# A software-pipelined FFT-and-MLP kernel: small products moved behind the next product with P, a group's swap moved behind the doubled copy

## The chip, the cores and the metric

The kernel runs on one core of a Trainium2 chip. Five engines have a part in it: TensorE (PE, with its weight loads shown as a row of their own, PEld), VectorE (DVE), ScalarE (ACT), GpSimd (POOL) and SyncE (SP), whose queue issues nearly all DMAs. The metric is the device time of one execution in microseconds; of several runs the median is taken. One run was also profiled, and its trace is what all durations here come from.

## The reference

Eight sequences of 3008 rows by 256 columns go through a two-dimensional FFT, of which the real part is kept; the result, 24064 rows, goes through a two-layer network with the gate `h * sigmoid(1.702 h)` between the layers.

```python
X = np.fft.fft(x, axis=1)          # x: (8, 3008, 256) float32
X = np.fft.fft(X, axis=2)
x = X.real.astype(np.float32).reshape(24064, 256)
h = x @ w_in                       # w_in: (256, 2048)
g = h * (1.0 / (1.0 + np.exp(-1.702 * h)))
out = (g @ w_out)                  # w_out: (2048, 256), all float32
```

## The kernel before, in words

**Tiles.** The FFT along the 3008 rows is split as 47 by 64. `fold1` (POOL, lines 225 to 231) adds mirrored halves of the input, `mix1` (PE, line 255) makes the 47-point transforms, `mixed` (ACT, line 263) copies their sums back into `xt`, `spill` and `fill` turn the data through memory, and `stage2` (PE, line 365, then DVE transposes, line 371) makes the 64-point part. The FFT along the 256 columns is folded into the weights `wcs`. What `stage2` leaves is `pqt[b, blk]`, with two halves, P (index 0) and Q (index 1). A row k and its mirror image share P and differ in the sign of Q, so both are had from one product with P and one with Q. Below, `mix1` and `stage2` together are called transforms.

**Steps and slots.** A step t is one quadruple (b, blk, hh, p): 8 sequences, 3 blocks of 512 rows, 2 halves of 256 rows (226 in the second half of the first block), and 8 pairs p of 128-wide chunks of the 2048 hidden features. There are 384 steps; the 8 steps of one (b, blk, hh) are a group, and each has its own output sums. The main loop (lines 989 to 1082) makes one pass, a slot, for each t. From t = 8 on, a slot issues on each engine the next piece of several steps at once, and the order in the source is the order in each engine's queue. There is no scheduler.

Slot t of the kernel before issues:

- On PE: `begin(t, 1)`, the product of step t with Q (line 184, `x`); the first part of the output product of step t - 3 (`product`, line 184, `o`); `begin(t + 1)`, the product of step t + 1 with P; the rest of the output product. Around these lie the small products (line 685): a second level of the fast 2-by-2 block product, made once for two steps. One slot of every two has those numbered 1, 2, 4, 7 (`one`), the other those numbered 5, 6, 3 (`other`).
- On ACT: `forward(t)` (line 607, the gate of the direct rows, from PSUM); in one slot of eight `swap` (lines 794 to 796, three copies of 64 partitions that exchange parts of a finished group's sums); `doubled(t + 1)` (line 604, the copy 2x of the product with P, before Q is added); `activate_back(t)` (line 614, the gate of the mirrored rows); `middle(t + 2)` (line 592, two activations that put the start value into the PSUM bank of x).
- On DVE: `backward(t)` (line 565, the mirrored rows, made from `doubled` and x); in odd or even slots `sums` (lines 629, 630) or `deeper` (line 651); and for a finished group `combine` (757, 758), `combine_small` (786), `combine_last` (768, 804) and two turns (737, each followed by stores on SP).
- On POOL: `sums(t, nc.gpsimd)` (lines 622, 623) and, where a slot has one, a part of `fold1`.

x has two PSUM banks, `b0` and `b1`, by the parity of t. A transform at the end of slot t borrows the bank of step t. It therefore has to wait for `forward(t)` and `backward(t)`, and `middle(t + 2)` cannot be issued in that slot: the code calls the slot `special`. The next slot, called `after`, starts with that `middle` on ACT, ahead of `forward`. There `begin(t + 1)` waits for a `middle` that was issued only a moment ago, and the kernel before puts three parts of the output product and the first small product in front of it. 51 slots are `after` slots. `begin(t, 1)` in turn waits for `doubled(t)`, which must have read the PSUM bank.

A group's last step is t0 with p = 7. In slot t0 + 3 `combine` runs, in t0 + 4 `combine_small`, in t0 + 5 (there the current step has p = 4) `swap` on ACT and `combine_last` on DVE, and in t0 + 6 and t0 + 7 the two turns with their stores. 46 groups have a swap.

The lines around the change:

```python
            product(t - LAG, 0, cut)
            if after:
                small_products(one[0], one[1][:1])
                small_products(other[0], () if opening else other[1][:1])
            if t + 1 < n:
                begin(t + 1)
...
            small_products(one[0], one[1][after:])
            swap(t - LAG - 2)
            if t < n:
                backward(t)
            if t + 1 < n:
                doubled(t + 1)
```

Of the kernel before, what the change touches and what calls it, by code (L numbers as in the profile page):

```python
# [43 lines left out]
LAG = 3  # L44
# [68 lines left out]
def kernel(ctx: ExitStack, tc, x, w_in, w_out, tab1, tab2, out):  # L113
# [471 lines left out]
    def middle(t):  # L585

        b, blk, hh, p = steps[t]
        n = width(t)
        x = xb[t] = bank("x", f"b{t % 2}")
        for i in range(2):  # L590
            f = 2 * p + i
            nc.scalar.activation(x[:, i * 256:i * 256 + n], nbt[b, blk][:, hh * 256:hh * 256 + n], ACTF.Copy,  # L592
                                 scale=af1[:, f:f + 1])
# [194 lines left out]
    def swap(t):  # L788

        if not group_end(t):  # L790
            return
        n = width(t)
        one, two_, kept = (free(big[lo:lo + 64], RES + at, [512, 2], [1, n]) for lo, at in ((64, 0), (0, 256), (64, 1024)))
        nc.scalar.copy(kept, two_)
        nc.scalar.copy(two_, one)
        nc.scalar.copy(one, kept)
# [192 lines left out]
    for t in range(n + LAG):  # L989
        if t < NP:  # L990
            if t == NP - 3:
                spare[:] = [tag for tag in spare if tag[0] == "o"] + ["b2"]
            if t == NP - 1:
                middle(NP)
            hidden(t)
            if t == NP - 1:
                begin(NP)
                no_row(1024)
            if t == 0:
                squares(in2, nc.scalar)  # L1000
                nyquist(0, 0)
                low_up(in2)
                low_down(in2)
            if t in rows_at:
                first_row(rows_at[t])
            if t >= LAG and t != LAG + 1:
                product(t - LAG, 0, None)
            if t == LAG:
                product(1, 0, None)
            if t == 5:  # L1010
                bounds(("out", 2))
            if t == 6:
                low_down(("out", 3))
            if t:
                activate(t - 1)
            if t == 3:
                bounds(("in", 3))
            if t == 5:
                bounds(("out", 3), False)
            if t in early:  # L1020
                fold_w(early[t])
            rows(t)
            if t == NP - 1:
                doubled(NP)
                middle(NP + 1)
        else:
            after, special = (any(fn in (mix1, stage2) for fn, _ in extra.get(k, ())) for k in (t - 1, t))
            if t < n:
                begin(t, 1)
            if t == NP:  # L1030
                activate(t - 1)
            if after and t + 1 < n:
                middle(t + 1)
            if t < n:
                forward(t)
            while waiting:
                m, ps = waiting.pop()
                mixed(m, 1, ps)
            opening = (t - LAG) % NP == 0 and t >= NP + LAG
            one, other = (t - LAG, (1, 2, 4, 7)), (t - LAG - 1, (5, 6, 3))  # L1040
            if opening:
                small_products(*other)
            cut = 0 if opening and not after else 3 if after else 2
            product(t - LAG, 0, cut)
            if after:
                small_products(one[0], one[1][:1])
                small_products(other[0], () if opening else other[1][:1])
            if t + 1 < n:
                begin(t + 1)
            if not opening:  # L1050
                small_products(other[0], other[1][after:])
            product(t - LAG, cut, 6 if t - LAG == last else None)
            small_products(one[0], one[1][after:])
            swap(t - LAG - 2)
            if t < n:
                backward(t)
            if t + 1 < n:
                doubled(t + 1)
            if t < n:
                activate_back(t)  # L1060
                sums(t, nc.gpsimd)
            if t + 2 < n and not special:
                middle(t + 2)
            combine_small(t - LAG - 1)
            if t - LAG == last:
                product(last, 6, None)
            sums(t - 1, nc.vector)
            deeper(t - 2, 0)
            deeper(t - 3, 1)
        if t == NP:  # L1070
            psu.close()
            low = ctx.enter_context(tc.tile_pool(name="low", bufs=1, space=PS))
            pot["low"] = low.tile([128, 3 * 512], F32, tag="low", name="low")
        if t >= LAG:
            combine(t - LAG)
            combine_last(t - LAG - 2)
            turn_last(t - LAG - 3, 0)
            turn_last(t - LAG - 4, 1)
        if t >= NP:
            spare[:] = [f"b{t % 2}"] * special + ["b2"]  # L1080
        for fn, args in extra.get(t, ()):
            fn(*args)
# [28 lines left out]
```

## Time and profile before

| | |
|---|---|
| median of 3 runs | 1855.01 us (1854.38 to 1855.89) |
| the profiled execution's own time | 1854.86 us |
| its span, first to last instruction | 1853.1 us |
| PE busy | 1836.6 us, 99% of the span |
| PEld busy | 1401.3 us, 76% |
| DVE busy | 1520.9 us, 82% |
| ACT busy | 1150.5 us, 62% |
| POOL busy | 975.2 us, 53% |
| granted TensorE clock, mean | 0.999 |

Busy time is the time in which an engine had at least one instruction under way. A line of the timeline gives the start in microseconds from the start of the span, the time from there to the end, the engine, the line of the source, the operation, the tiles written and read, the shape and the number of instructions put together; in brackets stands the idle time of the engine before it and what ended that. A line of the list of waits reads: who waited, for whom, microseconds in total, how often, the longest. fp32 matmuls are recorded in two passes, so that one `begin` of four matmuls shows as x8.

### The profile page before, as it was taken

Reading aid. Unit: us, or ns where it says so; the run is one execution under the profiler, and the core shown is the slowest. Engines: PE = TensorE matmul, PEld = TensorE weight load, DVE = VectorE, ACT = ScalarE, POOL = GpSimd, SP = SyncE. Lnnn points to the kernel's source line nnn. Section 1 sums busy time; section 2 is a strip of 40 time slices with the busy share of each in tenths; the row PEclk is TensorE's granted clock in tenths of the full one; section 3 lists DMA queues with packets and bytes.
Section 4 is the critical chain, followed back from the end, with each engine's and each line's share of the span. In section 5 each row is a group of like instructions: output and inputs, shape, how many; then the busy total and the mean of one; then the engine's idle time right before and its main releaser. Section 6 shows DMA issues by size and latency. Waiting matters only on the chain.

```text
span 1853.1 us, 56093 instructions
## 1 busy us (share of the span) xinstructions
PE 1836.6 (99%) x23722; PEld 1401.3 (76%) x23722; DVE 1520.9 (82%) x2222; ACT 1150.5 (62%) x2241; POOL 975.2 (53%) x1053
## 2 busy tenths in 40 slices
PE   8999999999999999999999999999999999999998
PEld 4677777777777777777777777777777777778776
DVE  6988778887798778987789878888888888878874
ACT  5666656665666666666566666666665666656663
POOL 4776446744368434773348643485445754444442
PEclk9999999999999999999999999999999999999999
DMA  8721340215012240223302132121411111100111
GB/s 280 181 61 34 85 67 19 72 52 99 19 46 48 73 81 13 52 50 90 57 13 67 43 86 52 19 75 35 103 31 23 37 46 36 31 19 13 23 19 24
DMA packets 149707, 105.31 MB, mean 57 GB/s; under 512 B 106057, under 2 KB 130665, under 8 KB 148896
## 3 DMA queue, kind: packets, MB, share of 16 engines
q1 hardware_dynamic: 146624, 99.68, 23.6%
q8 instruction: 187, 3.06, 0.7%
q10 hardware_dynamic: 2832, 2.05, 0.5%
q14 instruction: 64, 0.52, 0.1%
HBM read 64.41 MB, written 48.05 MB: 61 GB/s over the span
## 4 chain that ended last, share of the span: by engine, by line
PE 80%; DVE 9%; POOL 4%; ACT 2%; DMA 2%; issue 2%; SPq 0%; DVEq 0%; ACTq 0%; POOLq 0%
PE x L184 29%; PE o L184 22%; PE low L685 21%; PE o L685 3%; DVE big L651 3%; PE ps L255 2%; DVE big L786 2%; DVE big L565 1%; PE ps L365 1%; POOL xt L227 1%; DVE big L629 1%; POOL big L623 1%; DMA xt<-in_x_dram 1%; ACT big L607 1%; DMA Td<-big 1%
## 5 line engine op out<-in xcount | busy, mean ns | idle before, releaser
L622 POOL TENSOR_TENSOR big<-big 128x256 f32<-128x256 f32 (+1 forms) x376 | 353.0, 939 | 825.1 <-ACT big L614 691.4
L184 PE MATMUL x<-pq,wcs 128*64 128x256 f32 (+1 forms) x6016 | 768.8, 376 | 2.0 <-ACT g L604 1.4
L651 DVE TENSOR_TENSOR big<-big 128x512 f32<-128x512 f32 (+1 forms) x736 | 623.1, 861 | 23.4 <-PE low L685 4.7
L184 PE MATMUL o<-big,wo 128*64 128x256 f32 (+1 forms) x4800 | 620.8, 375 | 0.1
L184 PEld LDWEIGHTS x<-pq,wcs 128*64 128x64 f32 x6016 | 412.3, 137 | 186.0 <-issue 15.0
L184 PEld LDWEIGHTS o<-big,wo 128*64 128x64 f32 x4800 | 341.6, 137 | 148.0 <-DVE big L629 0.5
L604 ACT ACTIVATE g<-x 128x512 f32<-128x512 f32 (+1 forms) x376 | 221.6, 589 | 366.3 <-PE x L184 365.0
L565 DVE TENSOR_TENSOR big<-g,x 128x512 f32<-128x512 f32 (+2 forms) x440 | 254.1, 589 | 209.4 <-ACT big L607 209.0
L592 ACT ACTIVATE x<-nb,af 128x256 f32<-128x256 f32 (+1 forms) x752 | 352.9, 469 | 79.7 <-DVE pq L371 63.6
L685 PE MATMUL low<-big 128*64 128x128 f32 (+1 forms) x5888 | 382.8, 270 | 0.0
L685 PEld LDWEIGHTS low<-big 128*64 128x64 f32 x5888 | 337.5, 137 | 29.2
L623 POOL TENSOR_TENSOR big<-big 128x256 f32<-128x256 f32 (+1 forms) x376 | 352.6, 938 | 0.0
L607 ACT ACTIVATE big<-x 128x512 f32<-128x512 f32 (+1 forms) x376 | 219.2, 583 | 127.5 <-PE x L184 121.3
L614 ACT ACTIVATE big<-big 128x512 f32<-128x512 f32 (+1 forms) x376 | 231.9, 617 | 46.0 <-DVE big L565 44.0
L685 PE MATMUL low<-big,wo 128*64 128x128 f32 (+1 forms) x2944 | 220.4, 271 | 0.1
L685 PEld LDWEIGHTS low<-big,wo 128*64 128x64 f32 x2944 | 171.3, 137 | 4.2 <-DVE big L651 1.4
L630 DVE TENSOR_TENSOR big<-big 128x512 f32<-128x512 f32 (+1 forms) x188 | 160.8, 855 | 6.5
L629 DVE TENSOR_TENSOR big<-big 128x512 f32<-128x512 f32 (+1 forms) x188 | 137.3, 730 | 5.3 <-POOL big L622 5.3
L786 DVE TENSOR_TENSOR big<-big,low 128x512 f32<-128x512 f32 (+3 forms) x184 | 109.0, 609 | 3.5
L685 PEld LDWEIGHTS o<-big,wo 128*64 128x64 f32 x1472 | 92.2, 137 | 25.0
L685 PE MATMUL o<-big,wo 128*64 128x128 f32 (+1 forms) x1472 | 110.0, 270 | 0.0
L227 POOL TENSOR_TENSOR xt<-xt 111x510 f32<-111x510 f32 x56 | 86.0, 1535 | 4.4
(95 smaller groups left out, 966.2 us busy)
## 6 DMA issues: line engine op xcount, KB each, us to landing
out_dram<-os SPq DMA_DIRECT2D x284, 64.0 KB
t<-Td SPq DMA_DIRECT2D x22, 512.0 KB
Td<-xt SPq DMA_DIRECT2D x56, 192.0 KB
xt<-in_x_dram SPq DMA_DIRECT2D x14, 512.0 KB
xt<-Xr SPq DMA_DIRECT2D x14, 512.0 KB
nb<-Nd SPq DMA_DIRECT2D x23, 256.0 KB
out_dram<-os SPq DMA_DIRECT2D x96, 56.0 KB
Xr<-in_x_dram SPq DMA_DIRECT2D x7, 752.0 KB
```

The costliest lines, as they stand in the source:

```text
L184: nc.tensor.matmul(out[c0:c0 + 64], lhsT=lhs[:, c0:c0 + 64], rhs=rhs, skip_group_check=True, **how)
L565: nc.vector.tensor_tensor(free(out, at + m - 1, [by, 2], [RUN, blocks], [-1, m]), *ins, op=op)
L592: nc.scalar.activation(x[:, i * 256:i * 256 + n], nbt[b, blk][:, hh * 256:hh * 256 + n], ACTF.Copy, scale=af1[:, f:f + 1])
L604: nc.scalar.activation(two(g[:], n), two(xb[t][:], n), ACTF.Copy, scale=2.0)
L607: nc.scalar.activation(front(t), two(xb[t][:], width(t)), ACTF.Gelu_apprx_sigmoid)
L614: nc.scalar.activation(back(t), back(t), ACTF.Gelu_apprx_sigmoid)
L622: eng.tensor_tensor(right(t, S1, n), left(t, A21, n), right(t, A22, n), op=ALU.add)
L623: eng.tensor_tensor(left(t, S3, n), left(t, A11, n), left(t, A21, n), op=ALU.subtract)
L629: eng.tensor_tensor(s2, s1, a11, op=ALU.subtract)
L630: eng.tensor_tensor(s4, a12, s2, op=ALU.subtract)
L651: nc.vector.tensor_tensor(out, i0, i1, op=how)
L685: nc.tensor.matmul(o, lhsT=lhs, rhs=rhs, start=first_in, stop=(p == NP - 2), skip_group_check=True)
```

## The change

Three things are done. In `after` slots no small product stands between the output product and `begin(t + 1)` any more; all of them follow it. `swap` is issued later in the same slot, behind `doubled`, `activate_back` and, where the slot has it, `middle(t + 2)`. `combine_last` and both turns with their stores are issued one slot later: `combine_last` in the slot with p = 5, the turns in those with p = 6 and p = 7. Nothing is added or taken away.

```diff
@@ -1042,16 +1042,12 @@
             cut = 0 if opening and not after else 3 if after else 2
             product(t - LAG, 0, cut)
-            if after:
-                small_products(one[0], one[1][:1])
-                small_products(other[0], () if opening else other[1][:1])
             if t + 1 < n:
                 begin(t + 1)
             if not opening:
-                small_products(other[0], other[1][after:])
+                small_products(*other)
             product(t - LAG, cut, 6 if t - LAG == last else None)
-            small_products(one[0], one[1][after:])
-            swap(t - LAG - 2)
+            small_products(*one)
             if t < n:
                 backward(t)
             if t + 1 < n:
@@ -1061,6 +1057,7 @@
                 sums(t, nc.gpsimd)
             if t + 2 < n and not special:
                 middle(t + 2)
+            swap(t - LAG - 2)
             combine_small(t - LAG - 1)
@@ -1073,9 +1070,9 @@
         if t >= LAG:
             combine(t - LAG)
-            combine_last(t - LAG - 2)
-            turn_last(t - LAG - 3, 0)
-            turn_last(t - LAG - 4, 1)
+            combine_last(t - LAG - 3)
+            turn_last(t - LAG - 4, 0)
+            turn_last(t - LAG - 5, 1)
```

## The prediction

> **What bounds the kernel now.** I read the page first, then the list of waits, then the timelines of PE and ACT side by side around `after` slots and swaps, then DVE and POOL there.
>
> ```profile
> span 1853.1 us, 56093 instructions
> PE 1836.6 (99%) x23722; PEld 1401.3 (76%) x23722; DVE 1520.9 (82%) x2222; ACT 1150.5 (62%) x2241; POOL 975.2 (53%) x1053
> ...
> PEld x L184 <- ACT x L592: 8.6, 33, 0.7
> PEld x L184 <- ACT g L604: 4.0, 12, 0.5
> ```
>
> PE is the bound: its order is a string of matmuls of fixed pitch. So only a change in PE's stalls can move the time. Two kinds of stall touch the edits: `begin(t+1)` waiting for `middle` (L592) and `begin(t,1)` waiting for `doubled` (L604).
>
> I paired, for each slot, the first matmul of each begin with the end of the ACT instruction it needs. Where PE waits, it starts 0.05 us after that end; a distance of 0.10 already shows no wait. Counted from the pitch of the neighbours, PE loses 4.4 us in 36 slots to a late `doubled`: about 0.41 in each of six (PE near 368, 593, 818, 1043, 1267, 1492 us), 0.10 in six (near 336, 561, 786 ...), 0.05 to 0.06 in about sixteen, 0.28 and 0.15 once each, almost nothing in the rest. A load that could not be fetched ahead makes the second pair of matmuls late by another 0.05, so 36 x 0.05 = 1.8. **Together 6.2 us can be won.**
>
> A swap in an `after` slot (p = 4 behind a transform), PE:
>
> ```profile
> 367.36 1.04 PE L685 MATMUL low<-big 128*64 128x128 f32 x16
> 368.65 1.08 PE L184 MATMUL x<-pq,wcs 128*64 128x256 f32 x8 [0.24 <-ACT g L604]
> ```
>
> A swap in a `special` slot (t = 60, p = 4) with the `after` slot behind it; ACT, then PE, then DVE:
>
> ```profile
> 328.41 0.62 ACT L796 COPY big<-big 64x512 f32<-64x512 f32 x1
> 329.05 0.55 ACT L604 ACTIVATE g<-x 128x452 f32<-128x452 f32 x1
> 330.27 0.58 ACT L614 ACTIVATE big<-big 128x452 f32<-128x452 f32 x1 [0.67 <-DVE big L565]
> 332.03 0.59 ACT L263 COPY xt<-ps 128x512 f32<-128x512 f32 x1 [1.17 <-DMA Xr<-in_x_dram]
> 332.65 0.94 ACT L592 ACTIVATE x<-nb,af 128x226 f32<-128x226 f32 x2
> ```
>
> ```profile
> 332.69 1.31 PE L184 MATMUL o<-big,wo 128*64 128x226 f32 x12
> 333.83 0.56 PE L685 MATMUL low<-big 128*64 128x113 f32 x8
> 334.22 0.93 PE L184 MATMUL x<-pq,wcs 128*64 128x226 f32 x8
> ```
>
> ```profile
> 333.63 0.96 DVE L804 TENSOR_TENSOR big<-big 128x768 f32<-128x768 f32 x1
> 334.51 0.68 DVE L565 TENSOR_TENSOR big<-g,x 128x448 f32<-128x448 f32 x2
> 335.11 2.65 DVE L651 TENSOR_TENSOR big<-big 128x452 f32<-128x452 f32 x3
> 337.68 0.70 DVE L737 STREAM_TRANSPOSE os<-big 128x512 f32<-128x512 f32 x1
> 338.31 0.65 DVE L565 TENSOR_TENSOR big<-g,x 128x448 f32<-128x448 f32 x2
> ...
> 339.53 2.30 DVE L630 TENSOR_TENSOR big<-big 128x452 f32<-128x452 f32 x1
> ```
>
> To see: ACT has one idle stretch of 1.17 us between L614 and L263, the copy that frees the bank for `middle`; `begin` follows L592 by 0.64; DVE has no idle time at all.
>
> **The change part by part.** The sum is made against the profiled execution, 1854.86 us; the median of 1855.01 is 0.15 more.
>
> *1. Small product behind the begin.* Eight records of 128 columns take 0.43 us (0.36 at 113 columns), so in the 50 `after` slots that have it `begin(t+1)` comes that much sooner, as does `doubled(t+1)`. PE's work is the same. Distances from `middle` to begin there: 0.88, 0.68, 0.65 and 0.64; minus 0.43 or 0.36 they stay above 0.2: no wait. Six slots (b = 1 to 6, the first stage2 of a sequence; near 315, 540, 765 us) have 0.24 to 0.26: there begin waits 0.43 - 0.25 + 0.05 + 0.05 for the load = 0.28. **6 x 0.28 = +1.7.** The 36 stalls vanish: with the swap's part below, **-6.2**.
>
> *2. Swap behind `doubled`.* Three copies with gaps take 1.92 us (1.77 at 452 elements). In the plain slot ACT had idled 1.1 us for x anyway, so `doubled` was late by 0.83 and still in time. Now `forward(t+1)` queues behind the copies. Three cases.
>
> (a) Swap in a `special` slot. Now L604 runs ahead, L614 still waits for DVE's L565 and ends at 330.85, the copies fill 330.88 to 332.80, L263 starts at 332.83 instead of 332.03, L592 ends at 334.37 instead of 333.58. But begin is now wanted at 333.83, where the small product stood: a stall of 334.42 - 333.83 + 0.05 = 0.64. Six of these (b = 1 to 6): +3.8. For sequence 0 the same sum from its own rows (L614 ends at 141.56, copies to 143.36, L592 to 144.99, begin wanted at 144.19) gives 0.9, and the next one (near 183) 0.2. **+4.9.** Lower bound: each copy chain could be 0.1 shorter, 4.0.
>
> (b) Swap in an `after` slot (six; rows near 819 us). `doubled` is in time (its gain is in 1). `forward(t+1)` moves from 819.89 to 820.47: +0.58, and with it L565.
>
> (c) Plain swap (31; rows near 408 us). `forward` from 408.76 to 410.24; L565 was held by DVE until 411.34 and now starts at 410.86.
>
> *3. `combine_last` a slot later.* L768 and L804 leave the place before L565(p = 5) and stand before L565(p = 6). Behind L565 queue `activate_back` and `middle` on ACT, and begin(t+1) on PE one slot on. In (c): L565 410.86, three L651 to about 414.0, L768 and L804 (1.22 and 0.96) to 416.0; L565(p = 6) at 416.0 instead of 414.92; L614 to 417.28, `middle` to 418.15; begin wanted at 418.44. No wait, with 0.29 to spare. **0**; bounds 0 and, if one more POOL instruction gets ahead, 31 x 0.3 = 9.
>
> In (a): L565(61) starts at 334.9, three L651 end at 337.9, then L768 and L804, each held up by one POOL instruction of 0.65, to 340.6; L565(62) there instead of 338.31; L614 to 341.87; `middle` to 342.75. Begin is wanted at 341.66 plus the 0.41 that PE has lost = 342.07: 0.73 + 0.05. **6 x 0.78 = +4.7**; bounds 0 (no hold-up: L565(62) at 338.95) and 6 x 1.45 = 8.7 (POOL gets ahead twice, as L630 at 339.53 shows: 2.30 instead of 0.63).
>
> In (b): L565(166) at 827.0 instead of 825.38, `middle` to 829.2, begin wanted at 829.35 - 0.46 = 828.89: 0.36 + 0.05. **6 x 0.41 = +2.5**; bounds 0 and 6.6.
>
> One swap of 226 columns without a transform (near 1675 us): the stall of 0.34 at 1683.95 shrinks, a new one of about 0.9 comes a slot later: **+0.6**, bounds -0.3 and +1.
>
> Here a page bears on the case. The Trainium skill, "SBUF — State Buffer", Who interferes with whom, says that a DVE instruction with two SBUF inputs and a GpSimd instruction that reads SBUF exclude each other until the first has finished. By that rule a hold-up is one POOL instruction, as in +4.7; by the row of L630, where two more POOL instructions passed, it would be +8.7. That speaks against moving L768 and L804 to where POOL has `sums` and `fold1` back to back.
>
> *4. Turns and stores a slot later.* L737 (0.70) adds to DVE at p = 7 and leaves p = 5. The slots behind have idle DVE time (1.36 us ahead of L565 at 422.81), so 0; at most the plain bound above. On SP the stores are passed by the spill, row or fill DMAs of one slot; those then only start earlier, and each store has until its buffer comes round two groups later. All that any engine waited for a store before is 0.6 us: 0, from -0.6 to +0.6. The end of the kernel has a group without swap.
>
> Sum: -6.2 + 1.7 + 4.9 + 0 + 4.7 + 2.5 + 0.6 = +8.2; 1854.86 + 8.2 = 1863.1, with the median's 0.15 **1863.2 us**.
>
> **The rivals.**
>
> - *Only the direct waits* (items 1 and 2a; DVE catches up): -6.2 + 1.7 + 4.9 = +0.4, 1855.4. For it: DVE is idle 18% of the span. Against: not between p = 3 and p = 6.
> - *The gain alone.* If ACT's idle stretch of 1.17 us ahead of L263 took the whole swap, 2a would cost nothing, and with no lateness on DVE the time would be -6.2 + 1.7 = -4.5, 1850.5. It decides at 1.92 us of copies against 1.17 of room; only a swap that starts 0.75 earlier, so L565(60) earlier on DVE, would do it. Nothing here moves that.
> - *The DVE tail in every swap.* If L565(p = 6) is late by 0.3 more than worked out in (c), each of the 31 plain swaps stalls `begin` by up to 0.3: +8.2 + 9, 1872.
>
> **How the numbers follow.** Forecast 0.58, direct waits only 0.19, tail in every swap 0.15, gain alone 0.08. The forecast's own range is 1859 to 1869. A tenth is left out at each end: below, the direct waits with their lower bounds, 1854; above, the tail with the upper bounds of (a) and (b) in part, 1877. About 0.2% (3.7 us) is what a measurement of this kernel can tell from no change. Slower by more: the forecast but a twentieth, and the tail: 0.71. Within: the direct waits and that twentieth: 0.21. Faster: 0.08.
>
> **What would show it.** Right: PE waits for L604 nearly gone; waits of PEld for L592 up from 8.6 us to over 15; L263 near 332.8 directly behind L796; L565 waiting for L607 after swaps, and a begin at p = 7 of t = 63 that waits for L592. Wrong: waits for L592 unchanged (2a fails), or the DVE tail absent while begin at t = 62 still waits (item 3 fails). The prediction would be wrong as a whole if the contention of DVE and POOL falls out differently, since single instructions vary from 0.63 to 3.1 us by that alone.

## The result and the profile after

The changed kernel took **1863.97 us** (median of 6 runs, 1861.2 to 1865.52) against 1855.3 us (1854.38 to 1858.23) of the kernel before, run beside it: ratio 1.0042, 95% interval 1.0029 to 1.0055. It is slower by 8.7 us. The prediction said 1863.2 us. The total is right, but terms of the sum missed by several us each and partly cancelled; the experiments below are mostly about the two largest misses, the first stage2 slot and `mix1`.

The profiled execution of the changed kernel took 1861.7 us, 6.84 more than that of before. Its page, first lines:

```profile
span 1859.9 us, 56068 instructions
...
PE 1834.7 (99%) x23722; PEld 1402.3 (75%) x23722; DVE 1527.1 (82%) x2222; ACT 1153.2 (62%) x2241; POOL 1021.4 (55%) x1053
```

PE did the same work in nearly the same busy time (1836.6 before). POOL did the same work in 46 us more than before (975.2), and DVE in 6 us more, which fits instructions that hold each other up more often. From the list of waits (who waited, for whom, total us, how often, longest):

```profile
ACT big L614 <- DVE big L565: 98.1, 154, 1.7
...
PEld x L184 <- ACT x L592: 22.7, 26, 2.2
...
PE x L184 <- ACT x L592: 11.5, 16, 1.8
...
PEld x L184 <- ACT g L604: 0.3, 1, 0.3
```

The weight loads' wait for `doubled` (L604) is gone but for one of 0.3 us, as it was to be. The waits for `middle` (L592) grew from 8.6 to 22.7 us on PEld, and now PE itself waits for it too. (A PEld wait and a PE wait can be the same gap.) ACT waits for `backward` (L565) 98.1 us, where the list of the kernel before has:

```profile
ACT big L614 <- DVE big L565: 44.0, 70, 1.2
```

To see where PE lost time, the start of `begin(t, 1)` was compared slot by slot in the two traces. The distance grows by 6.84 us over the kernel, in these places. ("First stage2 slot" is the `after` slot behind the first `stage2` that is issued among the 48 steps of a sequence.)

| place | us, after against before |
|---|---|
| stalls for `doubled`, in slots with nothing else | -4.65 |
| first stage2 slot of six sequences (t = 57, 105, 153, 201, 249, 297) | +8.92 |
| `mix1` three slots on (t = 60 and so on) | -4.17 |
| `after` slot behind a special swap (t = 61 and so on), net of a stall of 0.155 that went there | +2.82 |
| t = 63 and so on | +1.73 |
| sequence 0, from its slot 8 on | +1.28 |
| from t = 336 on | +0.32 |
| opening, up to the first slot | +0.60 |

**The special swap.** ACT, then PE, of the changed kernel around t = 60, the place that the prediction showed near 330 us:

```profile
331.04 0.55 ACT L604 ACTIVATE g<-x 128x452 f32<-128x452 f32 x1 [0.98 <-PE x L184]
332.57 0.58 ACT L614 ACTIVATE big<-big 128x452 f32<-128x452 f32 x1 [0.99 <-DVE big L565]
333.18 0.62 ACT L794 COPY big<-big 64x512 f32<-64x512 f32 x1
...
334.48 0.61 ACT L796 COPY big<-big 64x512 f32<-64x512 f32 x1
335.12 0.59 ACT L263 COPY xt<-ps 128x512 f32<-128x512 f32 x1
335.74 0.94 ACT L592 ACTIVATE x<-nb,af 128x226 f32<-128x226 f32 x2
```

```profile
335.07 1.31 PE L184 MATMUL o<-big,wo 128*64 128x226 f32 x12
...
336.73 0.98 PE L184 MATMUL x<-pq,wcs 128*64 128x226 f32 x8 [0.34 <-ACT x L592]
```

The three copies now stand between L614 and L263, without the idle 1.17 us, and the begin waits for L592 ahead of the small product. By the pitch of the matmuls (their usual distance from start to start) PE loses 0.51 to 0.53 us there in each of the six sequences (the profile's own 0.34 counts from the modelled end of the matmul before).

**The tail on DVE,** two slots on (t = 61 and 62):

```profile
337.17 0.69 DVE L565 TENSOR_TENSOR big<-g,x 128x448 f32<-128x448 f32 x2 [2.42 <-ACT big L607]
337.78 2.29 DVE L651 TENSOR_TENSOR big<-big 128x452 f32<-128x452 f32 x3
339.98 1.15 DVE L768 TENSOR_TENSOR big<-big 128x512 f32<-128x512 f32 x1
341.17 1.36 DVE L804 TENSOR_TENSOR big<-big 128x768 f32<-128x768 f32 x1
342.46 0.68 DVE L565 TENSOR_TENSOR big<-g,x 128x448 f32<-128x448 f32 x2
```

L565 waits 2.42 us for `forward` behind the copies; L768 and L804 follow it. The begin at t = 63 loses 0.24 us, and the load 0.05.

**The plain swap** (slots 36 to 38), DVE:

```profile
224.44 0.69 DVE L565 TENSOR_TENSOR big<-g,x 128x512 f32<-128x512 f32 x1 [1.67 <-ACT big L607]
...
227.40 1.22 DVE L768 TENSOR_TENSOR big<-big 128x512 f32<-128x512 f32 x1
228.65 0.96 DVE L804 TENSOR_TENSOR big<-big 128x768 f32<-128x768 f32 x1
229.53 0.68 DVE L565 TENSOR_TENSOR big<-g,x 128x512 f32<-128x512 f32 x1
```

DVE of the kernel before, in the slots 36 and 37:

```profile
220.71 1.21 DVE L768 TENSOR_TENSOR big<-big 128x512 f32<-128x512 f32 x1
222.03 0.96 DVE L804 TENSOR_TENSOR big<-big 128x768 f32<-128x768 f32 x1
222.90 0.68 DVE L565 TENSOR_TENSOR big<-g,x 128x512 f32<-128x512 f32 x1
```

Here lies the core of the third part. In the kernel before, L768 and L804 stood ahead of the first of these L565, in the time in which it could not yet run. Now DVE idles there for 1.67 us, and the 2.2 us of L768 and L804 come behind it, where they delay the next L565. `middle` on ACT and the begin at p = 7 on PE, of the changed kernel:

```profile
230.78 0.97 ACT L592 ACTIVATE x<-nb,af 128x256 f32<-128x256 f32 x2
```

```profile
232.00 0.60 PE L184 MATMUL x<-pq,wcs 128*64 128x256 f32 x4
```

In 29 plain swaps `middle` ends 0.24 to 0.37 us before that begin starts (0.25 here), in one 0.54: no stall, and just barely.

**The first stage2 slot** (t = 57) is where the largest piece comes from. Three engines of the changed kernel, DVE first, then POOL, then PE; and behind them the same three of the kernel before in the same slot:

```profile
310.31 0.70 DVE L737 STREAM_TRANSPOSE os<-big 128x512 f32<-128x512 f32 x1
310.94 0.65 DVE L565 TENSOR_TENSOR big<-g,x 128x448 f32<-128x448 f32 x2
312.53 1.20 DVE L629 TENSOR_TENSOR big<-big 128x512 f32<-128x512 f32 x1 [0.94 <-POOL big L622]
...
315.92 1.43 DVE L371 STREAM_TRANSPOSE pq<-ps 128x256 f32<-128x256 f32 x4
```

```profile
305.11 1.17 POOL L622 TENSOR_TENSOR big<-big 128x256 f32<-128x256 f32 x1 [2.88 <-ACT big L614]
...
307.39 0.72 POOL L218 TENSOR_TENSOR e<-xt 47x254 f32<-47x254 f32 x1
...
310.54 1.28 POOL L227 TENSOR_TENSOR xt<-xt 111x510 f32<-111x510 f32 x1
311.76 0.74 POOL L622 TENSOR_TENSOR big<-big 128x256 f32<-128x256 f32 x1
```

```profile
314.41 0.98 PE L184 MATMUL x<-pq,wcs 128*64 128x226 f32 x8
...
317.80 0.98 PE L184 MATMUL x<-pq,wcs 128*64 128x226 f32 x8 [1.11 <-ACT x L592]
```

```profile
308.39 0.69 DVE L565 TENSOR_TENSOR big<-g,x 128x448 f32<-128x448 f32 x2 [0.64 <-ACT big L607]
309.61 1.20 DVE L629 TENSOR_TENSOR big<-big 128x512 f32<-128x512 f32 x1 [0.53 <-POOL big L622]
...
313.00 1.43 DVE L371 STREAM_TRANSPOSE pq<-ps 128x256 f32<-128x256 f32 x4
```

```profile
308.84 0.74 POOL L622 TENSOR_TENSOR big<-big 128x256 f32<-128x256 f32 x1
```

```profile
312.53 0.98 PE L184 MATMUL x<-pq,wcs 128*64 128x226 f32 x8
```

PE reaches this slot 1.88 us later than before (314.41 against 312.53), but L629 starts 2.92 later and L371, the transposes of `stage2` for which `middle` has to wait, also 2.92: 1.04 us of lateness of its own. Two queues lead there. On DVE the turn L737 fills the 0.64 us in which L565 used to wait. On POOL the late L565 makes L614 late, so L622 of slot 54 starts late, the first five instructions of `fold1` (L218 to L227, 4.4 us) stand behind it, the next L622 behind those, and L629 waits for that. Against PE, L565 is 0.66 us late and that L622 1.04; L629 starts right behind L622, so of the two queues POOL's is the one that ends last. The begin loses 1.27 or 1.28 us in four sequences and 1.91 or 1.92 in two; in these two L629 itself takes 1.90 and 1.89 us instead of 1.20, beside one POOL instruction more.

**`mix1` gives time back** (t = 60), which was in no term of the sum. The second of `sums` on DVE and POOL's instructions beside it, of the kernel before:

```profile
320.15 2.29 DVE L630 TENSOR_TENSOR big<-big 128x452 f32<-128x452 f32 x1
```

```profile
319.59 1.11 POOL L231 TENSOR_TENSOR xt<-xt 111x254 f32<-111x254 f32 x1
320.67 0.66 POOL L622 TENSOR_TENSOR big<-big 128x226 f32<-128x226 f32 x1
321.29 0.66 POOL L623 TENSOR_TENSOR big<-big 128x226 f32<-128x226 f32 x1
```

And of the changed one:

```profile
322.95 1.04 DVE L630 TENSOR_TENSOR big<-big 128x452 f32<-128x452 f32 x1
```

```profile
322.39 1.12 POOL L231 TENSOR_TENSOR xt<-xt 111x254 f32<-111x254 f32 x1
323.69 0.83 POOL L622 TENSOR_TENSOR big<-big 128x226 f32<-128x226 f32 x1 [0.18 <-ACT big L614]
```

Before, POOL ran L231, L622 and L623 there without a gap, and L630 took 2.29 us. Now POOL has to wait 0.18 us for L614 between L231 and L622, and L630 gets through in 1.04. What follows on DVE, as far as the L565 for which `mix1` waits, is earlier against PE. The kernel before shows that wait on PE:

```profile
330.39 0.29 PE L255 MATMUL ps<-e,w 47*64 47x129 f32 x1 [0.50 <-DVE big L565]
```

In the changed kernel it is gone in five sequences: 0.60 to 0.78 us each, and 0.18 in the slot ahead. In the sixth (t = 251 and 252) L630 took 1.04 us before as well, and nothing is given back.

### The profile page after: what moved, and what is told of

Same layout as the page of the kernel before. It is cut to its first block, busy times and chain, and to the rows that moved or that the text cites. A ratio compares the mean times of both kernels' runs of the same rounds, so it can differ in the third digit from the quotient of the medians.

```text
span 1859.9 us, 56068 instructions
## 1 busy us (share of the span) xinstructions
PE 1834.7 (99%) x23722; PEld 1402.3 (75%) x23722; DVE 1527.1 (82%) x2222; ACT 1153.2 (62%) x2241; POOL 1021.4 (55%) x1053
## 4 chain that ended last, share of the span: by engine, by line
PE 82%; DVE 8%; ACT 3%; issue 2%; DMA 2%; POOL 2%; SPq 0%; ACTq 0%; DVEq 0%; POOLq 0%
PE x L184 31%; PE o L184 23%; PE low L685 22%; PE o L685 4%; DVE big L651 2%; ACT x L592 1%; DVE big L565 1%; PE ps L255 1%; PE ps L365 1%; DVE big L786 1%; DMA xt<-in_x_dram 1%; DVE big L449 1%; DMA Td<-big 0%; POOL big L623 0%; DVE big L804 0%
## 5 line engine op out<-in xcount | busy, mean ns | idle before, releaser
L622 POOL TENSOR_TENSOR big<-big 128x256 f32<-128x256 f32 (+1 forms) x376 | 378.4, 1006 | 785.4 <-ACT big L614 642.7
L651 DVE TENSOR_TENSOR big<-big 128x512 f32<-128x512 f32 (+1 forms) x736 | 646.1, 895 | 20.1 <-PE low L685 3.0
L184 PEld LDWEIGHTS x<-pq,wcs 128*64 128x64 f32 x6016 | 416.5, 137 | 201.5 <-ACT x L592 22.7
L604 ACT ACTIVATE g<-x 128x512 f32<-128x512 f32 (+1 forms) x376 | 221.8, 590 | 357.0 <-PE x L184 356.7
L565 DVE TENSOR_TENSOR big<-g,x 128x512 f32<-128x512 f32 (+2 forms) x440 | 254.0, 589 | 216.7 <-ACT big L607 216.6
L592 ACT ACTIVATE x<-nb,af 128x256 f32<-128x256 f32 (+1 forms) x752 | 352.5, 469 | 89.9 <-DVE pq L371 55.9
L685 PE MATMUL low<-big 128*64 128x128 f32 (+1 forms) x5888 | 377.6, 270 | 0.0
L623 POOL TENSOR_TENSOR big<-big 128x256 f32<-128x256 f32 (+1 forms) x376 | 374.9, 997 | 0.0
L614 ACT ACTIVATE big<-big 128x512 f32<-128x512 f32 (+1 forms) x376 | 232.2, 618 | 99.8 <-DVE big L565 98.1
L630 DVE TENSOR_TENSOR big<-big 128x512 f32<-128x512 f32 (+1 forms) x188 | 139.3, 741 | 6.5
L629 DVE TENSOR_TENSOR big<-big 128x512 f32<-128x512 f32 (+1 forms) x188 | 134.7, 716 | 7.3 <-POOL big L622 7.3
L227 POOL TENSOR_TENSOR xt<-xt 111x510 f32<-111x510 f32 x56 | 75.3, 1345 | 4.4
```

What stands on the lines that cost most here:

```text
L184: nc.tensor.matmul(out[c0:c0 + 64], lhsT=lhs[:, c0:c0 + 64], rhs=rhs, skip_group_check=True, **how)
L565: nc.vector.tensor_tensor(free(out, at + m - 1, [by, 2], [RUN, blocks], [-1, m]), *ins, op=op)
L604: nc.scalar.activation(two(g[:], n), two(xb[t][:], n), ACTF.Copy, scale=2.0)
L614: nc.scalar.activation(back(t), back(t), ACTF.Gelu_apprx_sigmoid)
L622: eng.tensor_tensor(right(t, S1, n), left(t, A21, n), right(t, A22, n), op=ALU.add)
L623: eng.tensor_tensor(left(t, S3, n), left(t, A11, n), left(t, A21, n), op=ALU.subtract)
```

## The experiments

All kernels ran beside the kernel before, whose median there was 1855.07 to 1855.66 us; each ratio, and each difference to the kernel before, is to that. Two kernels of different runs are compared by their differences to it. "Places" are the rows of the table above, from each kernel's own trace. Behind the opening, whose time no edit touches but which is 0.64 us shorter to 4.57 longer than before in the profiled executions, the traces give the same differences as the medians to within 1 us, but for one kernel: the changed kernel is 6.2 us behind by its trace and 8.7 by its median. So a difference to the changed kernel is given by both; the one of the medians may be some 2 us too large.

### The two halves of the change, each alone

The small products alone behind the begin; swap, last sums and turns as before:

```diff
 # against the changed kernel
+            swap(t - LAG - 2)
             if t < n:
                 backward(t)
...
-            swap(t - LAG - 2)
...
-            combine_last(t - LAG - 3)
-            turn_last(t - LAG - 4, 0)
-            turn_last(t - LAG - 5, 1)
+            combine_last(t - LAG - 2)
+            turn_last(t - LAG - 3, 0)
+            turn_last(t - LAG - 4, 1)
```

> The small products behind the begin alone; swap, combine_last and the turns stand as before. Theory (the cost of the change comes from the swap and what follows it on DVE, not from the order of the small products): most stalls of begin(t,1) for L604 go (six of 0.10, some sixteen of 0.055 and the 0.05 behind each), the six of 0.41 stay, and in the first stage2 slot of a sequence begin waits for L592 by about 0.28: together 2 to 4 us faster than before. Rival (the new wait of 1.3 to 1.9 us in the first stage2 slot comes from the begin standing 0.43 earlier): that wait stays at over 1 us in six slots, and the time is 3 us or more above before.

Measured: 1851.8 us (1850.59 to 1856.26, 10 runs), ratio 0.9983, interval 0.9973 to 0.9992. So this half is a gain of 3.3 us. Its first stage2 slots wait 0.22 to 0.28 us, 1.44 in all six (the prediction's own 1.7 for the small products), and `mix1` gives back 3.36 already here: 4.16 in the five sequences of the change, less 0.80 in the sixth, where L630 now takes 2.29 us instead of 1.04.

The other half alone, small products as before:

```diff
 # against the changed kernel
+            ahead = after
+            if ahead:
+                small_products(one[0], one[1][:1])
+                small_products(other[0], () if opening else other[1][:1])
             if t + 1 < n:
                 begin(t + 1)
             if not opening:
-                small_products(*other)
+                small_products(other[0], other[1][ahead:])
             product(t - LAG, cut, 6 if t - LAG == last else None)
-            small_products(*one)
+            small_products(one[0], one[1][ahead:])
```

> Swap, combine_last and turns moved as in the change; the small products stay ahead of the begin. Theory: the first stage2 slot of a sequence still has a wait for L592 of about 0.85 (1.28 less the 0.43 that the small product fills), the slot behind a swap in a special slot 0.15, the stalls of 0.41 are gone: 2 to 8 us slower than before. Rival (order of the small products): no slower than before, minus 2.7 for the stalls of 0.41 that go.

Measured: 1867.6 us (1867.43 to 1870.74, 4 runs), ratio 1.007, interval 1.0055 to 1.0085: 12.5 us slower, more than either theory gave. Places: first stage2 +6.3, t = 63 and so on +3.12, special swaps +1.34, no give-back at `mix1` (+0.87), and +1.40 at t = 71 and so on, behind the swaps in `after` slots, which the whole change has not. By the medians the two halves add up, 12.5 - 3.3 = 9.2 against the 8.7 of the whole change; place by place they do not, so that is partly chance. The small products alone gain, so the loss of the change is in the swap's half.

The last sums and turns a slot later, with the swap and the small products as before:

```diff
 # against the kernel before
-            combine_last(t - LAG - 2)
-            turn_last(t - LAG - 3, 0)
-            turn_last(t - LAG - 4, 1)
+            combine_last(t - LAG - 3)
+            turn_last(t - LAG - 4, 0)
+            turn_last(t - LAG - 5, 1)
```

> combine_last and both turns with their stores a slot later; swap stays ahead of doubled and the small products as before. Theory (DVE is late because forward, and so L565, queue behind the swap; without that DVE catches up, since L565 at p = 5 is then free at once): within 2 us of before, no new wait for L592 in the first stage2 slot. Rival (the turn that is added at p = 7, or the stores a slot later on SP, make the wait by themselves): waits of 0.7 us or more in those six slots, 4 us or more slower.

Measured: 1856.44 us (1855.78 to 1857.57), ratio 1.0006, interval 0.9996 to 1.0016. Moved alone, last sums and turns cost nothing that can be told. (In one of the six sequences, at t = 153, the first stage2 slot did lose 0.97 us: there L630 took 2.35 us instead of 1.10.) Together with the later swap they cost 12.5; the swap moved alone was not tried, so this does not divide the loss between the two. It shows only that the later sums do little harm by themselves.

### Which swap the first stage2 wait comes from

The change, but the last group of each sequence, whose swap lies four slots ahead of the first stage2, keeps its old slots:

```diff
 # against the changed kernel; the same condition for last sums and turns (g % 48 != 47)
+            swap_late = (t - LAG - 2) % 48 != 47
+            if not swap_late:
+                swap(t - LAG - 2)
             if t < n:
                 backward(t)
...
-            swap(t - LAG - 2)
+            if swap_late:
+                swap(t - LAG - 2)
```

> As the change, but the last group of each sequence (the one ahead of the first stage2 of the next) has its swap, combine_last and turns at the old places. Theory: the wait for L592 in the first stage2 slot falls from 1.28 or 1.9 to about 0.28; but mix1 four slots on again waits for L565 by about 0.6, as before the change, so that of the 1.0 to 1.6 won in each of six sequences some 0.8 are given back: 1 to 5 us faster than the change, 4 to 7 us slower than before. Rival (the wait in that slot is additive): 6 to 9 us faster than the change, level with before.

Measured: 1854.23 us (1853.21 to 1857.34), ratio 0.9996, interval 0.9987 to 1.0006: level with the kernel before, and 9.6 us under the changed kernel by the medians (0.9 under the kernel before, the change 8.7 over it), 7.5 by the traces. The theory that had it 4 to 7 us slower than before is wrong; the additive rival, 6 to 9 us, fits. First stage2 falls from +8.92 to +1.44; `mix1` keeps its -4.14, special swaps (+2.81) and t = 63 (+1.72) stay as they were. DVE of this kernel in slot 57:

```profile
309.29 0.69 DVE L565 TENSOR_TENSOR big<-g,x 128x448 f32<-128x448 f32 x2 [0.66 <-ACT big L607]
310.48 1.21 DVE L629 TENSOR_TENSOR big<-big 128x512 f32<-128x512 f32 x1 [0.50 <-POOL big L622]
```

The idle 0.66 and the short wait of 0.50 are those of the kernel before. So 7.5 of the 8.9 us come from one group in each sequence, whose swap, sums and turns are the last ahead of `fold1` and `stage2`. That also shows that the give-back at `mix1` does not come from that wait, since it stays without it.

### What the special swaps cost

```diff
 # against the changed kernel
+            swap_late = not special
+            if not swap_late:
+                swap(t - LAG - 2)
             if t < n:
                 backward(t)
...
-            swap(t - LAG - 2)
+            if swap_late:
+                swap(t - LAG - 2)
```

> As the change, but in special slots the swap stays ahead of doubled. Theory: the wait of 0.53 for L592 behind those slots (0.85 in sequence 0) goes, that of 0.24 two slots later too, and nothing else changes: 4 to 6 us faster than the change. Rival (the stall only moves, since doubled is late again): 0 to 1 us.

Measured: 1858.21 us (1856.73 to 1862.55), ratio 1.0017, interval 1.0008 to 1.0027: 5.5 us under the changed kernel by the medians, 3.1 by the traces. The special swaps fall from +2.82 to -0.63 and sequence 0 from 1.28 to 0.08, 4.65 us together; this term was the prediction's +4.9. But "nothing else changes" did not hold. The begin at t = 63 waits no longer, yet `mix1` in the same slot now waits for L565 instead (+2.06 at t = 63 and so on, 1.73 in the change). And in the first stage2 slot (+10.16 instead of +8.92) L629 takes 1.89 us or more in four sequences, not in two.

### How near the plain swaps are to a stall

The change with both turns in their old slots, the first of them directly behind `combine_last` at p = 5, so that DVE has one L737 of 0.70 us more ahead of L565 at p = 6:

```diff
 # against the changed kernel
-            turn_last(t - LAG - 4, 0)
-            turn_last(t - LAG - 5, 1)
+            turn_last(t - LAG - 3, 0)
+            turn_last(t - LAG - 4, 1)
```

> As the change, but the turns keep their old slots, p = 5 (directly behind combine_last) and p = 6. One more L737 of 0.70 then stands ahead of L565 at p = 6 after each swap. Theory (after a plain swap the begin at p = 7 has only 0.24 to 0.29 to spare): a wait for L592 of 0.4 to 0.5 appears in each of some 30 plain groups, 8 to 15 us slower than the change, while the wait in the first stage2 slots shrinks. Rival (DVE at p = 6 has slack): 2 to 5 us faster than the change, because the turn at p = 7 is gone.

Measured: 1890.65 us (1889.27 to 1892.74, 4 runs), ratio 1.019, interval 1.0176 to 1.0204: 27 us slower than the change (28.3 by the traces), nearly twice the upper end of the theory's 8 to 15. PE at p = 7 of a plain swap (slot 39):

```profile
232.38 0.65 PE L184 MATMUL x<-pq,wcs 128*64 128x256 f32 x4 [0.29 <-ACT x L592]
```

By the pitch this begin is 0.46 us late, and it is late in every one of the 30 plain swaps, by 0.40 to 0.46 in 29 of them: roughly the 0.70 of the turn less what was left (0.46 where 0.25 were left, 0.41 where 0.28 to 0.37 were). With a weight load that is late behind it, 0.46 to 0.58 us a slot, 16.0 us in all. The other places grow as well: first stage2 +12.49 instead of +8.92, t = 63 and so on +6.04 instead of +1.73. The rival of the prediction, "the DVE tail in every swap", was thus a quarter to a third of a microsecond of DVE time away.

### Two hybrids

Small products behind the begin everywhere; swap, last sums and turns late only where the swap falls in an `after` slot, which are the six groups with the large stall for `doubled`:

```diff
 # against the changed kernel; last sums and turns by the same six groups
+            swap_late = after
+            if not swap_late:
+                swap(t - LAG - 2)
             if t < n:
                 backward(t)
...
-            swap(t - LAG - 2)
+            if swap_late:
+                swap(t - LAG - 2)
```

> Small products behind the begin everywhere; swap, combine_last and turns moved only for the six groups whose swap falls into an after slot, the others as before. Theory: all stalls for L604 go, those of 0.41 included (6 x 0.46), and only the first stage2 slots wait for L592, by 0.28: 4 to 6 us faster than before. Rival (contention of DVE and POOL brings a new wait in those groups): no faster than x1.

Measured: **1850.29 us** (1849.41 to 1854.38, 11 runs), ratio 0.9975, interval 0.9966 to 0.9984. It beats both kernels, and is the fastest of the study. Its profiled execution was the longest of the eleven, with 4.6 us more than before in the opening, ahead of slot 8; behind that it is 5.1 us shorter than the one of before. By its places, the stalls for `doubled` go (-4.6), first stage2 costs 1.46, `mix1` gives back 3.37. One loss was not expected: in four slots (t = 94, 206, 318, 374) a begin waits for L592, 0.34 to 0.48 us each, 1.51 in all. In the slot before each of them DVE idles 0.46 us between L768 and L804, instead of the 0.10 where the small products alone are moved; what holds L804 is not known.

To save that 1.46, the small product was put back ahead of the begin in the first stage2 slot alone:

```diff
 # against the hybrid
             product(t - LAG, 0, cut)
+            ahead = after and t % 48 == 9 and t >= 48
+            if ahead:
+                small_products(one[0], one[1][:1])
+                small_products(other[0], () if opening else other[1][:1])
...
-                small_products(*other)
+                small_products(other[0], other[1][ahead:])
...
-            small_products(*one)
+            small_products(one[0], one[1][ahead:])
```

> As x7, with the small product left ahead of the begin in the first stage2 slot of sequences 1 to 7. Theory: the waits of 0.28 there go as well: another 1 to 1.7 us faster, 5 to 7 us faster than before. Rival (the waits there let DVE catch up and are paid back at mix1): level with x7.

Measured: 1852.68 us (1851.83 to 1854.77), ratio 0.9988, interval 0.9979 to 0.9996: slower than the hybrid by 2.4, which neither the theory (faster) nor the rival (level) had. The wait went, as expected (first stage2 +0.02), but the give-back went with it (`mix1` +0.05 instead of -3.37) and was the larger of the two. DVE of this kernel at the place shown above:

```profile
320.81 2.29 DVE L630 TENSOR_TENSOR big<-big 128x452 f32<-128x452 f32 x1
```

L630 is back at 2.29 us, in the same five sequences as before. So the small product's place in the first stage2 slot decides, by way of when POOL and DVE meet, over 0.6 to 0.8 us at `mix1` three slots later.

### The two queues of the first stage2 slot

Is it POOL's queue? The first piece of `fold1` was moved: its instructions for `e` two slots, the next two one slot ahead. The same move was made in the hybrid and, as a control, in the kernel before.

```diff
-        if c == 0 and part == 0:
+        if part < 0:
...
+            return
...
+            ahead = 0 if late else 2
+            at(t0 + 6 + late - ahead, fold1, b + 1, 0, -1, nc.gpsimd)
             for c in range(NCH):
                 for part in range(2):
-                    at(t0 + 6 + 2 * c + part + late, fold1, b + 1, c, part, nc.gpsimd)
+                    by = ahead // 2 if c + part == 0 else 0
+                    at(t0 + 6 + 2 * c + part + late - by, fold1, b + 1, c, part, nc.gpsimd)
```

> Edit: the whole change, and in the six sequences after the first transform group's, the first piece of fold1 is taken out of the slot t = 54: its three instructions for e (L218 to L220) are issued two slots sooner and the next two (L225, L227) one slot sooner. Work and results are the same. Theory (the wait of 1.27 to 1.92 us in the first stage2 slot is a queue on POOL: L622 of slot 54 comes 1.1 us later than before because L614 waits for a later L565, five fold1 instructions of 4.4 us stand behind it, and L622 of slot 55, for which DVE's L629 waits 0.94, behind those): with the five instructions gone L629 has nothing to wait for, the first stage2 waits fall to 0.3 or less, and the time falls by 6 to 9 us from the changed kernel, to 1855 to 1858. Rival (DVE itself is late, by L768, L804 and L737 a slot later, and POOL is late only because DVE is): L629 starts as late as now, the waits stay at 1.3 and 1.9, and the time is the changed kernel's, 1862 to 1866.

> Edit: the kernel with the small products behind the begin and swap, last sums and turns late only for the six groups whose swap is in an after slot, and the first piece of fold1 two slots and one slot sooner. Theory: the 0.22 to 0.28 us that the first stage2 slot still waits there go, because L629 no longer waits 0.5 for POOL's L622; 6 x 0.28 = 1.7 us less than without the fold's move, 1848.5. Rival (the give-back at mix1 three slots on, 0.6 to 0.8 in five sequences, hangs on where POOL's L622 and L630 fall against each other, and moves with the fold): it is lost, and the time is 1850.3 - 1.7 + 4 = 1852.6.

> Edit: the kernel before, with only the first piece of fold1 two slots and one slot sooner: the control for the other two. There begin of the first stage2 slot has 0.24 to 0.26 us to spare and waits for nothing, so the theory expects no gain: 1855, within 2 us. Rival: the moved instructions contend with DVE's backward and sums in the slots 52 and 53, and middle is late there: 3 to 5 us slower.

Measured: the change with it 1860.24 us (1859.26 to 1862.51, 10 runs; ratio 1.0024, interval 1.0014 to 1.0034), so 4.0 us less than the change by the medians and 0.9 by the traces, where the theory had 6 to 9 and the rival 0. The theory is wrong, and by the traces the rival is near. In these kernels every line from the new `return` on has a number one higher. DVE of the change with the move:

```profile
311.13 0.70 DVE L630 TENSOR_TENSOR big<-big 128x512 f32<-128x512 f32 x1
311.87 2.35 DVE L631 TENSOR_TENSOR big<-big 128x512 f32<-128x512 f32 x1
...
314.75 1.43 DVE L372 STREAM_TRANSPOSE pq<-ps 128x256 f32<-128x256 f32 x4
```

The first of `sums` (L630 here) waits for POOL no longer, as the theory had it. It still starts 0.66 us late against PE, behind a DVE without pause. Then the second (L631) takes 2.35 us instead of 1.10, and the begin still waits 1.11 to 1.13 us. Take away POOL's queue, and a busy DVE that meets POOL's instructions is what is late next. (1.13 us are lost in the slot before as well, t = 56 and so on, where the change loses nothing.)

The hybrid with the move: 1852.92 us (1852.45 to 1855.08, 10 runs; ratio 0.9988, interval 0.9979 to 0.9998). Its first stage2 wait is gone, as the theory said, and `mix1` keeps its give-back (-4.16), against the rival; but the moved instructions cost 0.33 and 0.58 us in the slots 54 and 55, six times each, which neither theory nor rival had. So the time is the rival's 1852.6 and not the theory's 1848.5, but not for the rival's reason. The control: 1856.2 us (1855.45 to 1861.89, 10 runs; ratio 1.0009, interval 0.9999 to 1.0018), no difference that can be told, as expected, but made of two parts, +5.5 in the slots 54 and 55 and -4.19 at `mix1`. So the give-back can be had without moving any small product, too: it hangs on how POOL's and DVE's instructions meet.

Is it the turn? The change with the first piece of `fold1` moved, and without the second turn of each sequence's last group, which removes the L737 that is new at p = 7 there and leaves that part of the output unwritten:

```diff
 # against the change with the first piece of fold1 moved
-        if group_end(t):
+        if group_end(t) and (t % 48, half) != (47, 1):
             turned(t, pot["out"], half, oc[:, 2 * half:])
```

> Edit: the changed kernel with the first piece of fold1 two slots and one slot sooner, and the second turn (one L737 at p = 7) with its stores left out for the last group of each sequence; this part of the output is not written. In the run with the fold moved, L629 waits for POOL no longer and DVE is busy without a pause from 302.4 to 316.1 us, and the first stage2 slot still waits 1.1 us. Theory (the turn a slot later is the second bound there: it takes the 0.64 us in which DVE waited for L607 in the kernel before): L565 of slot 57 and L629 come 0.6 us sooner and L630 falls clear of POOL's L622, so that the wait falls from 1.1 to between 0 and 0.5: 4 to 7 us faster than with the turn, 1853 to 1856. Rival (only the way in which L630 and POOL's instructions fall against each other matters, and it stays passed by two of them): the wait stays near 1.1, and the time is within 1.5 us of 1860.2.

Measured: 1860.52 us (1859.63 to 1862.22, 8 runs), ratio 1.0027, interval 1.0016 to 1.0038. The rival holds: no gain. DVE:

```profile
312.81 2.41 DVE L631 TENSOR_TENSOR big<-big 128x512 f32<-128x512 f32 x1
```

Half of the theory came true: L630 starts 0.6 us sooner against PE, where it stood in the kernel before (to within 0.05). But L631 is still passed by POOL's instructions, L652 behind it takes 1.15 us instead of 0.68, the first stage2 waits are still 1.02 or 1.03, and the place costs 6.12 instead of 6.70. So the turn is not the bound by itself either.

What is settled: the wait in the first stage2 slot comes from the move of swap, last sums and turns in the group ahead of it, by way of a DVE and a POOL that are both without pause from there on. POOL's queue ends last in the changed kernel, the turn accounts for 0.6 us on DVE, and with both gone the begin waits nearly as long for a DVE instruction that POOL's pass. What stays open: how the wait divides between the three. Taking away one cause at a time brought another forward each time.

## Why the prediction was right, and where it was not

- **The stalls for `doubled` go, -6.2.** Right: one wait of 0.3 us is left of 5.4 on PE and PEld together. PE's busy time moved by 0.1%.
- **Item 1, small products, +1.7.** Right in itself: 1.44 where the small products alone are moved, 0.22 to 0.28 a slot against 0.28.
- **Item 2a, special swaps, +4.9.** Right: 0.51 to 0.53 and 0.05 for the load a slot against 0.64, 0.85 at t = 21 against 0.9, and 4.65 us in these places by the run that undoes it.
- **Item 3(c), plain swaps, 0 with 0.29 to spare.** Right at the begin of p = 7: no stall in any of 30, 0.24 to 0.37 left in 29. The run with the turns back shows that 0.70 more on DVE turns into a stall of 0.40 to 0.46.
- **Items 3(c) and 4 failed behind six of them.** The prediction put the turns' 0.70 at 0 because "the slots behind have idle DVE time", from a row near 422 us, and closed (c) at the begin of p = 7. It did not follow the same lateness into the slots behind a sequence's last group, where DVE's idle time is 0.64 and not 1.36, where POOL has the first piece of `fold1` queued, and where DVE's next work is the transposes of `stage2`. The mis-sized term is the first stage2 slot: 8.9 measured against 1.7. The missing 7.2 lies behind the swaps that the run with the last groups as before puts back.
- **The time given back at `mix1`, -4.2, was in no term.** The prediction read the 2.29 us of L630 as a bound of a cost. It was also a loss of the kernel before, which a small shift of POOL against DVE could undo.
- **Item 3(a), +4.7: too large.** 1.7 measured (0.24 and 0.05 a slot against 0.78). L565 at t = 61 came where the sum had it (334.8 in the time of before, against 334.9). But the three L651 behind it took 2.2 us as far as the start of L768 where the sum had 2.4, and L768 and L804 took 2.5 where it had 2.7 with a POOL instruction ahead of each. So L565 of t = 62 came at 340.1 in the time of before, not at 340.6.
- **Item 3(b), +2.5: did not come.** No begin there waits; 0.31 us are left at t = 167. That was inside its bounds, 0 to 6.6. In the swap's half alone it did come, with 0.23 us in each of six.
- **The 226-wide swap, +0.6.** Right in size: the stall of 0.34 shrank to 0.15, the new one a slot later is 0.52, and with the loads it is 0.5 in all.
- **The stores, 0.** Nothing in the changed trace speaks against it.

By the traces the misses are +7.2, -4.2, -3.0 and -2.5; they cancel to -2.5, and with small rests the profiled difference is 6.84 where the sum said 8.2. The medians differ by 8.7, and 1.8 us of that is in no place of the two traces. That the forecast of 1863.2 stands 0.8 from the median is luck to that extent. Of the rivals, "only the direct waits" falls with the first stage2 slot, "the gain alone" with the special swaps, and "the tail in every swap" by 0.24 us of room.

The prediction weighed a rule of the Trainium skill ("SBUF — State Buffer", Who interferes with whom: a DVE instruction with two SBUF inputs and a GpSimd instruction that reads SBUF exclude each other until the first is done). The trace agrees in (a), where L804 took 1.36 us instead of 0.96. The prediction read from the rule that a hold-up is one POOL instruction. That reading the traces do not bear out: L630 at 2.29, and L631 above at 2.35 and 2.41, lie beside two or three of POOL's instructions in a row.

## What to carry to other kernels

When a step is moved out of one engine's idle time, follow its lateness on every engine that waits for it up to the next place where two queues are full, and make the sum from the rows of that place, not from those of a like one. Split a change of several parts by running each alone: here the small products' move was worth 3.3 us and that of swap, sums and turns cost 12.5, and keeping the second only for the six groups that had the stall made a kernel 4.8 us faster than before. A margin of 0.24 to 0.37 us in 29 places is worth knowing before the next edit: 0.70 us of DVE time ate it, and with the other waits that it lengthened cost 27.

## What had not been expected of the hardware

Back-to-back POOL instructions can pass a waiting DVE instruction more than once. L630 (128 by 452, two inputs) took 2.29 us while POOL ran L231, L622 and L623 without a gap, and 1.04 us when POOL paused 0.18 us between the first two; alone it takes 0.63. At this place the traces have these two lengths and no other: 2.28 to 2.30 us in five of six sequences of the kernel before and of the hybrid with the first slot put back and in all six of the swap's half alone; 1.04 in all six of the change and in five of the small products alone and of the hybrid. Wherever L630 changes from the one to the other, `mix1` gains or loses its 0.6 to 0.8 us. So a reordering on PE by 0.4 us moved the time by 0.6 to 0.8 us three slots on, through engines that it did not touch.
